# A decode step on one core: VectorE's program as a loop, and one weight load in two parts

## The chip, the core and the metric

The kernel runs on one core of a Trainium2 chip. TensorE (PE) multiplies, VectorE (DVE), ScalarE (ACT) and GpSimd (POOL) work on the operands, and SyncE (SP) issues nearly all DMAs. 16 DMA engines carry the data. The metric is the device time of one execution in microseconds: the median of the kernel before is 292.82 us over three runs (292.77 to 292.93).

## The reference

One decode step of a transformer block for two sequences with one token each, D = 640. x is normalised and multiplied by w_q into 32 heads of 192. Each head attends to the last 2048 of 8192 cached positions, the result goes through w_o, and a feed-forward block with a tanh GELU follows; both blocks add to the residual. Everything is bf16.

```python
W = min(4096, max(256, Sk // 4))                      # 2048
q = (layernorm(x) @ wq).reshape(B, 1, 32, 192).transpose(0, 2, 1, 3)
k, v = k_cache[:, :, Sk - W:, :], v_cache[:, :, Sk - W:, :]
p = softmax(einsum("bhqd,bhkd->bhqk", q, k) * 192 ** -0.5)
h = x + einsum("bhqk,bhkd->bhqd", p, v).transpose(0, 2, 1, 3).reshape(B, 1, 6144) @ wo
n = layernorm(h)
out = h + (gelu(n @ w_gate) * (n @ w_up)) @ w_down
```

Nearly all of the 122 MB that it reads are keys and values (2 x 32 heads x 2048 x 192 x 2 bytes, twice), w_q and w_o. Each byte is used once.

## The kernel before

**Groups.** The 64 pairs of a sequence and a head are worked through in 16 groups of four (g = 0 to 15). A group's keys are one load of 3 MB, its values another, both into a ring of six slots in SBUF. For a group PE transposes the keys in six batches into PSUM (`transposes`, L546), and VectorE (four batches, L573) and ScalarE (two, L569) copy them to `ktr`. Then come the scores (L616) into the PSUM bank `sps`, VectorE's masking and row maximum (L628), its product with a selection (L632), PE's product that spreads the maximum (L635), VectorE's negated maximum `nm` (L637), ScalarE's exponential (L639), PE's turn of the exponentials into columns (L646), VectorE's masked copy of them to `ering` (L653) and PE's product with the values (`pv`, L658). After four groups, a pass J, the sums are divided and multiplied by that pass's quarter of w_o (`z_rows`, `o_rows`, `o_columns`, `oproj`). The products of passes 0 and 1 go to `hrow`: the first by a copy (L723), the second by an addition (L725).

**The tail.** After group 15, `oproj(3)` gives the residual h, PE and VectorE normalise it, and the feed-forward block follows: w_gate (L832, L834), the GELU on VectorE (L835 to L845), w_up in two loads of four and one row blocks (`WUC`, L846), the product `uT` (L850), and w_down in four loads (`WDC`, L851 to L862). VectorE copies the result to `yrow` (L863) and SP writes it out.

**Loads and their order.** `load` puts a load in a queue and `pump` (L336) issues from the head of the queue as soon as the ring slots that it overwrites have been used (`done`). All loads of the ring go through SP in one fixed order: k0, w_q, k1, v0, k2, v1, and so on, w_o's quarters in between, then w_gate, w_up, w_down. The first block of w_gate and x go through ScalarE's queue.

**Order and waits.** `_Prog` records each operation with what it reads and writes, and `resolve` (L129) works out the semaphore waits. PE's program between the first scores and the last group is a loop of four trips, one for a pass (`emit_loop`, L188), in which a wait's value is a constant plus a stride times the trip; parts that do not occur in every pass stand under a condition ("oc", "op", "d0" to "d2"). VectorE has two semaphores (`cls` 0 and 1), so that these strides are constant. The programs of VectorE, ScalarE, GpSimd and SP are written out without a loop. Three calls of `addr_align` (L876, L878, L881) put the next instruction of GpSimd's, VectorE's and ScalarE's program at a chosen place in a block of 128 instructions: place 0, 120 and 0.

The lines that set this:

```python
WUC = ((0, 4), (4, 5))
P.resolve({("dve", 0): 4 * 8, ("dve", 1): 8, ("act", 0): 4 * 3, ("pool", 0): 4})
nc.vector.addr_align(128, 120, 2)
P.emit("dve", nc.vector, sems)
```

Of the kernel before, what the change touches and what calls it, by code (L numbers as in the profile page):

```python
# [6 lines left out]
F32 = mybir.dt.float32  # L7
# [7 lines left out]
NC5 = D // 128  # L15
# [4 lines left out]
F = 1536  # L20
# [3 lines left out]
SCALE = DH ** -0.5  # L24
GELU_2C = 2.0 * 0.7978845608028654


# [23 lines left out]
class _Prog:  # L51
# [3 lines left out]
    def __init__(self):  # L55
        self.ops = []
        self.per = {}
        self.count = {}
        self.w = {}
        self.r = {}  # L60
        self.x = {}
        self.dma_count = {}
        self.seg = self.trip = None
        self.seg_n = 0

    def loop_seg(self, seg=None, trip=None):
        self.seg, self.trip, self.seg_n = seg, trip, 0

    def op(self, eng, fn, R=(), W=(), X=(), dma=None, cls=0):
        o = _Op(eng, cls, fn)  # L70
        deps = []

        def add(y, same_ok):
            if y is None or y is o:
                return
            if y.dma_sem is None and y.eng == eng and dma is None and same_ok:
                return
            deps.append(y)

        for t in R:  # L80
            add(self.w.get(t), eng == "pe")
        for t in W:
            add(self.w.get(t), eng == "pe")
            for y in self.r.get(t, ()):
                add(y, True)
        for t in X:
            for e, y in self.x.get(t, {}).items():
                if e != eng:
                    add(y, True)
        for t in R:  # L90
            self.r.setdefault(t, []).append(o)
        for t in W:
            self.w[t] = o
            self.r[t] = []
        for t in X:
            self.x.setdefault(t, {})[eng] = o
        if dma is not None:
            o.dma_sem = dma
            self.dma_count[dma] = self.dma_count.get(dma, 0) + 16
            o.dma_val = self.dma_count[dma]  # L100
        o.deps = deps
        k = (eng, cls)
        self.count[k] = self.count.get(k, 0) + 1
        o.idx = self.count[k]
        if eng == "pe" and self.seg is not None:
            o.seg, o.slot, o.trip = self.seg, (self.seg, self.seg_n), self.trip
            self.seg_n += 1
        self.per.setdefault(eng, []).append(o)
        self.ops.append(o)
        return o  # L110

    def resolve(self, strides):
# [25 lines left out]
        body = {}  # L138
# [13 lines left out]
        for e, l in self.per.items():  # L152
            n = {}
            for o in l:
                if o.dma_sem is None:
                    n[o.cls] = n.get(o.cls, 0) + (1 if o.need_inc else 0)
                    o.inc_val = n[o.cls]
        self.body = []
        made, at = {}, {}
# [4 lines left out]
        for slot, l in body.items():  # L164
            waits = []
            for key, by in need.get(slot, {}).items():
                S = 16 if key[0] == "d" else strides[key]
                a = max((y.dma_val if y.dma_sem is not None else y.inc_val) - S * t for t, y in by.items())
                for o in l:
                    v = a + S * o.trip  # L170
                    assert 0 < v <= at[slot, o.trip].get(key, 0), (slot, key, o.trip, v, at[slot, o.trip].get(key))
                waits.append((key, a, S))
            self.body.append((l[0].seg, l[0].slot[1], l[0], waits))

# [12 lines left out]

    def emit_loop(self, eng, sems, trips, order):  # L188
        l = self.per["pe"]
        inside = [k for k, o in enumerate(l) if o.slot is not None]  # L190
        self.emit("pe", eng, sems, l[:inside[0]])
        bodies = {}
        for seg, n, o, waits in self.body:
            bodies.setdefault(seg, []).append((n, o, waits))
        with eng.Fori(0, trips) as i:
            def put(items):
                for item in items:
                    if isinstance(item, tuple):
# [7 lines left out]
                        continue  # L206
                    for n, o, waits in sorted(bodies.pop(item), key=lambda q: q[0]):
                        self.emit_one(o, eng, sems, [(key, S * i + a if S else a) for key, a, S in waits])
            put(order)
        assert not bodies, list(bodies)  # L210
        self.emit("pe", eng, sems, l[inside[-1] + 1:])


GRAN = 256
SLOT = 24576
RING = 6 * SLOT
TPG = 64
WDC = ((0, 6), (6, 9), (9, 11), (11, 12))
WUC = ((0, 4), (4, 5))
# [8 lines left out]
def bass_sequential_preLN__sliding_block_cached__geglu_ffn__decode_kernel(  # L228
# [12 lines left out]
    with ExitStack() as ctx:  # L241
# [56 lines left out]
        mrhs = sb("mrhs", [128, 16], BF16)  # L298
        sm = sb("sm", [128, 512], F32)
        nm = sb("nm", [128, 1], F32)  # L300
        zr = sb("zr", [128, 4], F32)
# [30 lines left out]

        def load(key, off, nbytes, src, shape, sem):
            queue.append((key, off, nbytes, src, shape, sem))

        def pump():  # L336
            while queue:
                key, off, nbytes, src, shape, sem = queue[0]
                old = [q for q in live if q[1] < off + nbytes and off < q[1] + q[2]]
                if any(q[0] not in used for q in old):  # L340
                    return
                for q in old:
                    live.remove(q)
                queue.pop(0)
                live.append((key, off, nbytes))
                v = shape(ring[:, off // 2:(off + nbytes) // 2])
                toks = [("ring", x) for x in range(off // GRAN, (off + nbytes + GRAN - 1) // GRAN)]
                where[key] = (v, toks)
                P.op("sp", lambda e, v=v, src=src: e.dma_start(v, src), W=toks + [("sem", sem)], dma=sem)  # L349
# [32 lines left out]
        def load_ffn():  # L382
            load(("wg", 1), K_AT[1], 2 * (NC5 - 1) * F, B_w_gate.rearrange("(p c) f -> p c f", c=NC5)[:, 1:NC5, :],
                 lambda v: v.rearrange("p (c f) -> p c f", f=F), "wg1")
            for i, (c0, c1) in enumerate(WUC):
                load(("wu", i), K_AT[3] + 2 * c0 * F, 2 * (c1 - c0) * F, B_w_up.rearrange("(p c) f -> p c f", c=NC5)[:, c0:c1, :],
                     lambda v: v.rearrange("p (c f) -> p c f", f=F), f"wu{i}")
            wd = B_w_down.rearrange("(q p s) n -> q p s n", p=128, s=6)
# [11 lines left out]

        def pe(fn, R=(), W=(), X=()):
            return P.op("pe", fn, R, W, X)

# [40 lines left out]
        dve(lambda e: e.memset(xnT[:, :, :].rearrange("p a b -> p (a b)").bitcast(I32), 0), W=["xnT"])  # L444
        dve(lambda e: e.memset(lsx[:, :, :], 0.0), W=["lsx"])
        dve(lambda e: e.memset(sps[:, :], 0.0), X=["s"])
        dve(lambda e: e.memset(m1[:, :], 0.0), X=["m1"])
# [128 lines left out]
        def q_rows():  # L576
# [10 lines left out]

            pe(fn, R=["xnT"] + wtoks, X=[("t", 0)])
            done("wq")
# [5 lines left out]
        def q_stationary():  # L595
# [8 lines left out]

            pe(fn, R=["qrow", "selq"], X=["o"])
            dve(lambda e: e.tensor_copy(qs[:, :], ops_[:, 0:384]), W=["qs"], X=["o"])  # L606
# [9 lines left out]
        def scores(g):  # L616
# [9 lines left out]
            if g + 4 < NG:  # L626
                q_masked(g + 4)
            dve(lambda e: e.tensor_tensor_reduce(  # L628
                out=sm[:, :].rearrange("p (u x) -> p u x", u=4), in0=sps[:, :].rearrange("p (u x) -> p u x", u=4),
# [4 lines left out]
        def softmax(g):  # L634
# [4 lines left out]
            act(lambda e: e.activation(out=eexp[:, :], in_=sm[:, :], func=ACT.Exp, bias=nm[:, 0:1], scale=1.0,  # L639
                                       accum_out=zr[:, g % 4:g % 4 + 1]), R=["nm", "sm"],  # L640
                W=["eexp", ("zr", g % 4)])
# [61 lines left out]
        def oproj(J):  # L703
            for i, (k0, k1) in enumerate(wo_parts(J)):
# [16 lines left out]
                done(("wo", J, i))  # L721
            if J == 0:
                dve(lambda e: e.tensor_copy(hrow[0:98, :], m1[0:98, 192:512]), W=["hrow"], X=["m1"])  # L723
            if J == 1:
                dve(tt(hrow[0:98, :], m1[0:98, 192:512], hrow[0:98, :], ALU.add), R=["hrow"], W=["hrow"], X=["m1"])  # L725
# [141 lines left out]

        P.resolve({("dve", 0): 4 * 8, ("dve", 1): 8, ("act", 0): 4 * 3, ("pool", 0): 4})
        sems = {}
        for e, c in (("pe", 0), ("act", 0), ("dve", 0), ("dve", 1), ("pool", 0)):  # L870
            sems[e, c] = ctx.enter_context(nc.semaphore(f"s_{e}{c}"))
        for d in P.dma_count:
            sems["d", d] = ctx.enter_context(nc.semaphore(f"s_{d}"))
        P.emit("sp", nc.sync, sems)
        nc.sync.wait_ge(sems["d", "dout"], 16)
        nc.gpsimd.addr_align(128, 0, 2)  # L876
        P.emit("pool", nc.gpsimd, sems)
        nc.vector.addr_align(128, 120, 2)  # L878
        P.emit("dve", nc.vector, sems)
        P.emit("act", nc.scalar, sems, P.per["act"][:2])  # L880
        nc.scalar.addr_align(128, 0, 2)  # L881
        P.emit("act", nc.scalar, sems, P.per["act"][2:])
        P.emit_loop(nc.tensor, sems, 4, ["a0", (0, None, ["oc"]), "a1", (0, 3, ["op"]), "a2", "b0", "b1", "b2", "c0", "c1", "c2",
                                         (None, 3, ["d0", "d1", "d2"])])

# [27 lines left out]
```

## Time and profile before

| | |
|---|---|
| median of three runs | 292.82 us |
| the profiled execution | 292.81 us |
| its span, first to last instruction | 291.5 us |
| DMA in the span | 122.45 MB, 420 GB/s |
| PE, VectorE, ScalarE, GpSimd busy | 68%, 42%, 26%, 9% |
| mean granted TensorE clock | 0.872 |

The profile is one execution. Busy shares are of the span. The two lines of digits for DMA and GB/s cut the span into 40 equal slices; a DMA digit is the mean busy share of the 16 DMA engines in tenths. Queue q1 is SP's, q10 ScalarE's; "instruction" marks packets that carry program code. The trace also holds each DMA packet by itself, with its queue, size, start and duration, though not the engine that carried it.

### The profile page before, as it was taken

Reading aid. Unit: us, or ns where it says so; the run is one execution under the profiler, and the core shown is the slowest. Engines: PE = TensorE matmul, PEld = TensorE weight load, DVE = VectorE, ACT = ScalarE, POOL = GpSimd, SP = SyncE. Lnnn points to the kernel's source line nnn. Section 1 sums busy time; section 2 is a strip of 40 time slices with the busy share of each in tenths; the row PEclk is TensorE's granted clock in tenths of the full one; section 3 lists DMA queues with packets and bytes.
Section 4 is the critical chain, followed back from the end, with each engine's and each line's share of the span. In section 5 each row is a group of like instructions: output and inputs, shape, how many; then the busy total and the mean of one; then the engine's idle time right before and its main releaser. Section 6 shows DMA issues by size and latency. Waiting matters only on the chain.

```text
span 291.5 us, 4909 instructions
## 1 busy us (share of the span) xinstructions
PE 198.8 (68%) x2141; PEld 147.6 (51%) x2141; DVE 123.1 (42%) x215; ACT 76.9 (26%) x72; POOL 25.4 (9%) x84
## 2 busy tenths in 40 slices
PE   0560858887677377849577478868478778496684
PEld 0450427566375274728374475645465746473341
DVE  5250025455416345535356243635247445253331
ACT  1050013343323122513222123523142334151001
POOL 7820064000000000000000000000000000000000
PEclk9997578999959989997989679999689899788857
DMA  8999999999999999999999999999999999999994
GB/s 311 449 422 428 434 428 432 427 431 428 427 420 442 428 432 432 428 432 432 432 419 444 432 426 432 432 428 432 432 428 432 432 432 428 432 425 414 422 417 172
DMA packets 6507, 122.45 MB, mean 420 GB/s; under 512 B 734, under 2 KB 864, under 8 KB 1504
## 3 DMA queue, kind: packets, MB, share of 16 engines
q1 hardware_dynamic: 6348, 121.90, 97.7%
q10 hardware_dynamic: 148, 0.40, 0.5%
q8 instruction: 7, 0.11, 0.2%
q14 instruction: 4, 0.03, 0.0%
HBM read 122.29 MB, written 0.00 MB: 420 GB/s over the span
## 4 chain that ended last, share of the span: by engine, by line
DMA 63%; PE 24%; DVE 9%; SPq 1%; ACT 1%; issue 1%; POOL 0%; DVEq 0%
DMA ring<-in_A_k_cache_dram 44%; PE tpp L559 16%; DMA ring<-in_A_wq_dram 10%; DMA ring<-in_B_w_down_dram 9%; DVE ktr L573 7%; PE tpp L583 2%; PE sps L620 2%; PE ops L664 2%; SPq L349 1%; DVE ering L414 1%; DVE sm L628 1%; ACT ktr L569 1%; PE m L715 1%; PE m L697 1%; DVE mrhs L410 0%
## 5 line engine op out<-in xcount | busy, mean ns | idle before, releaser
L559 PE MATMUL tpp<-identf,ring 128*128 128x128 f32 x768 | 116.5, 314 | 40.2 <-DMA ring<-in_A_k_cache_dram 26.7
L559 PEld LDWEIGHTS tpp<-identf,ring 128*128 128x128 f32 x768 | 102.9, 163 | 48.6 <-DMA ring<-in_A_k_cache_dram 27.5
L573 DVE COPY ktr<-tpp 128x2048 bf16<-128x2048 bf16 x64 | 78.3, 1224 | 92.5 <-PE tpp L559 92.3
L569 ACT ACTIVATE ktr<-tpp 128x2048 bf16<-128x2048 bf16 x32 | 60.1, 1877 | 95.8 <-PE tpp L559 95.8
L639 ACT ACTIVATE eexp<-sm,nm 128x512 bf16<-128x512 f32 x16 | 11.5, 722 | 72.0 <-DVE nm L637 72.0
L620 PE MATMUL sps<-ktr,rq 128*16 128x512 bf16 x384 | 25.7, 401 | 1.1 <-POOL rq L414 1.1
L664 PE MATMUL ops<-ring,ering 128*32 128x384 bf16 x512 | 25.0, 340 | 0.0
L628 DVE CUSTOM_DVE_ANT_1 sm<-sps,mska 128x512 f32<-128x512 f32 x16 | 11.1, 691 | 27.0 <-PE sps L620 27.0
L414 POOL TENSOR_TENSOR rq<-qs,mask 128x96 bf16<-128x96 bf16 x16 | 5.6, 356 | 175.7 <-PE sps L620 153.6
L664 PEld LDWEIGHTS ops<-ring,ering 128*32 128x32 bf16 x512 | 12.7, 99 | 8.5 <-issue 2.0
L620 PEld LDWEIGHTS sps<-ktr,rq 128*16 128x16 bf16 x384 | 8.8, 89 | 14.3 <-issue 5.4
L635 PEld LDWEIGHTS m<-mrhs,pm 128*128 128x128 bf16 x16 | 1.5, 96 | 23.0 <-DVE mrhs L410 23.0
L635 PE MATMUL m<-mrhs,pm 128*128 128x16 bf16 x16 | 2.9, 184 | 14.9 <-DVE mrhs L410 14.9
L583 PE MATMUL tpp<-ring,xnT 128*32 128x384 bf16 x80 | 6.2, 502 | 9.1 <-DMA ring<-in_A_wq_dram 9.1
L583 PEld LDWEIGHTS tpp<-ring,xnT 128*32 128x32 bf16 x80 | 3.4, 144 | 11.8 <-issue 9.4
L414 DVE TENSOR_TENSOR ering<-m,mask 128x256 bf16<-128x256 f32 x16 | 6.6, 414 | 1.3 <-PE m L648 1.3
L606 DVE CAST qs<-ops 128x384 bf16<-128x384 f32 x1 | 0.6, 556 | 15.6 <-PE ops L601 15.6
L697 PE MATMUL m<-selb,orow 128*128 128x2 bf16 x48 | 3.5, 199 | 5.3 <-DVE ering L414 4.6
L697 PEld LDWEIGHTS m<-selb,orow 128*128 128x128 bf16 x48 | 3.1, 161 | 6.0 <-DVE ering L414 5.0
L648 PE MATMUL m<-sel,eexp 128*128 128x64 bf16 x64 | 4.6, 196 | 1.2 <-ACT eexp L639 1.2
L414 DVE TENSOR_TENSOR orow<-m,wm 128x1536 bf16<-128x1536 f32 x3 | 5.3, 1750 | 0.0
L648 PEld LDWEIGHTS m<-sel,eexp 128*128 128x128 bf16 x64 | 4.3, 102 | 1.6 <-DVE nm L637 1.3
(126 smaller groups left out, 89.1 us busy)
## 6 DMA issues: line engine op xcount, KB each, us to landing
ring<-in_A_k_cache_dram SPq DMA_DIRECT2D x16, 3072.0 KB, 29.4
ring<-in_A_v_cache_dram SPq DMA_DIRECT2D x16, 3072.0 KB, 25.1
ring<-in_A_wq_dram SPq DMA_DIRECT2D x1, 7680.0 KB, 28.7
ring<-in_A_wo_dram SPq DMA_DIRECT2D x4, 1920.0 KB, 21.5
ring<-in_B_w_gate_dram SPq DMA_DIRECT2D x1, 1536.0 KB, 31.2
ring<-in_B_w_up_dram SPq DMA_DIRECT2D x1, 1536.0 KB, 21.9
ring<-in_B_w_down_dram SPq DMA_DIRECT2D x1, 960.0 KB, 24.3
ring<-in_B_w_down_dram SPq DMA_DIRECT2D x1, 480.0 KB, 25.0
```

Of the source, the lines that this page charges most:

```text
L414: return lambda e: e.tensor_tensor(out=out, in0=a, in1=b, op=op)
L559: ins = e.transpose(tpp[bi][:, 512 * j + 128 * u:512 * j + 128 * (u + 1)], kv[:, off:off + 128], identf[:, :])
L569: act(lambda e, dst=dst, bv=bv: e.activation(out=dst, in_=bv, func=ACT.Copy), W=[("kt", half, k)], X=both)
L573: dve(lambda e, dst=dst, bv=bv: e.tensor_copy(dst, bv.rearrange("p (a x) -> p a x", a=2)), W=[("kt", half, k)], X=both, cls=0)
L583: ins = e.matmul(tps[0][32 * r:32 * (r + 1), 0:384], lhsT=xnT[:, c, 32 * J:32 * (J + 1)], rhs=wq[:, c, 1536 * J + 384 * r:1536 * J + 384 * ...
L620: ins = e.matmul(sps[32 * ch:32 * ch + 16, :], lhsT=rq[:, g % 4, k, :], rhs=ktr[:, k // 2, 1024 * ch + k % 2:1024 * (ch + 1):2], start=(k ...
L628: dve(lambda e: e.tensor_tensor_reduce(out=sm[:, :].rearrange("p (u x) -> p u x", u=4), in0=sps[:, :].rearrange("p (u x) -> p u x", u=4), ...
L635: pe(lambda e: e.matmul(m2[:, 256:272], lhsT=pm[:, :], rhs=mrhs[:, :], start=True, stop=True), R=["pm", "mrhs"], X=["m2"])
L639: act(lambda e: e.activation(out=eexp[:, :], in_=sm[:, :], func=ACT.Exp, bias=nm[:, 0:1], scale=1.0, accum_out=zr[:, g % 4:g % 4 + 1]), R= ...
L648: ins = e.matmul(o, lhsT=eexp[:, 128 * u:128 * (u + 1)], rhs=sel64[:, :], start=True, stop=True)
L664: ins = e.matmul(ops_[32 * r:32 * (r + 1), 0:384], lhsT=ering[:, g % 4, t, :], rhs=vv[:, 384 * t:384 * (t + 1)], start=(g % 4 == 0 and t < 4),
L697: ins = e.matmul(m2[:, 2 * kk:2 * kk + 2], lhsT=orow[:, :, kk:DH:12], rhs=selb[:, :], start=True, stop=True)
```

## The change

VectorE's program gets a loop of four trips like PE's, and the three `addr_align` calls leave. For the loop each of VectorE's operations must be the same in every trip. So the first addition to `hrow` is an addition too, on a `hrow` that GpSimd sets to zero at the start. A small memset (`gate`) ahead of L628 takes the wait for the scores, and the exponential waits for `gate` as well. PE's operations that do not occur in every trip get a semaphore of their own (`cls` 1).

The second load of w_up (one row block of 128 partitions, 384 KB) becomes two loads, first partitions 100 to 127, then 0 to 99, each with its own semaphore. PE's four products with it wait for both.

```diff
+LOOPED = ("pe", "dve")
+RARE = ("oc", "op")
...
     def op(self, eng, fn, R=(), W=(), X=(), dma=None, cls=0):
+        if eng == "pe" and self.seg in RARE:
+            cls = 1
...
-        if eng == "pe" and self.seg is not None:
-            o.seg, o.slot, o.trip = self.seg, (self.seg, self.seg_n), self.trip
-            self.seg_n += 1
+        if eng in LOOPED and self.seg is not None:
+            n = self.seg_n.get(eng, 0)
+            o.seg, o.slot, o.trip = self.seg, (eng, self.seg, n), self.trip
+            self.seg_n[eng] = n + 1
...
+        for l in body.values():
+            for o in l:
+                if o.eng == "pe" and o.need_inc and o.trip > l[0].trip:
+                    n = (o.inc_val - l[0].inc_val) // (o.trip - l[0].trip)
+                    assert strides.setdefault(o.key(), n) == n, (o.key(), n)
...
+WUP = 100
...
+        gate = sb("gate", [128, 1], F32)
...
+        def part_toks(off, nbytes, part):
+            return [("ring", x, part) for x in range(off // GRAN, (off + nbytes + GRAN - 1) // GRAN)]
...
+                if part is not None:
+                    P.op("sp", lambda e, v=v, src=src: e.dma_start(v, src), W=part_toks(off, nbytes, part) + [("sem", sem)], X=toks, dma=sem)
+                    continue
...
-                load(("wu", i), K_AT[3] + 2 * c0 * F, 2 * (c1 - c0) * F, B_w_up.rearrange("(p c) f -> p c f", c=NC5)[:, c0:c1, :],
-                     lambda v: v.rearrange("p (c f) -> p c f", f=F), f"wu{i}")
+                off, nb = K_AT[3] + 2 * c0 * F, 2 * (c1 - c0) * F
+                src = B_w_up.rearrange("(p c) f -> p c f", c=NC5)[:, c0:c1, :]
+                if i == 0:
+                    load(("wu", i), off, nb, src, lambda v: v.rearrange("p (c f) -> p c f", f=F), f"wu{i}")
+                    continue
+                for p0, p1 in ((WUP, 128), (0, WUP)):
+                    load(("wu", i), off, nb, src[p0:p1], lambda v, p0=p0, p1=p1: v[p0:p1, :].rearrange("p (c f) -> p c f", f=F),
+                         f"wu{i}{p0}", p0)
...
+        pool(lambda e: e.memset(hrow[:, :], 0.0), W=["hrow"])
...
+            dve(lambda e: e.memset(gate[:, :], 0.0), W=["gate"], X=["s"], cls=0)
...
-                                       accum_out=zr[:, g % 4:g % 4 + 1]), R=["nm", "sm"],
+                                       accum_out=zr[:, g % 4:g % 4 + 1]), R=["nm", "sm", "gate"],
...
-            if J == 0:
-                dve(lambda e: e.tensor_copy(hrow[0:98, :], m1[0:98, 192:512]), W=["hrow"], X=["m1"])
-            if J == 1:
+            if J < 2:
                 dve(tt(hrow[0:98, :], m1[0:98, 192:512], hrow[0:98, :], ALU.add), R=["hrow"], W=["hrow"], X=["m1"])
...
-        P.resolve({("dve", 0): 4 * 8, ("dve", 1): 8, ("act", 0): 4 * 3, ("pool", 0): 4})
+        P.resolve({("dve", 0): 4 * 9, ("dve", 1): 8, ("act", 0): 4 * 3, ("pool", 0): 4})
...
-        nc.gpsimd.addr_align(128, 0, 2)
         P.emit("pool", nc.gpsimd, sems)
-        nc.vector.addr_align(128, 120, 2)
-        P.emit("dve", nc.vector, sems)
-        P.emit("act", nc.scalar, sems, P.per["act"][:2])
-        nc.scalar.addr_align(128, 0, 2)
-        P.emit("act", nc.scalar, sems, P.per["act"][2:])
...
+        P.emit("act", nc.scalar, sems)
+        order = ["a0", (0, None, ["oc"]), "a1", (0, 3, ["op"]), "a2", "b0", "b1", "b2", "c0", "c1", "c2", (None, 3, ["d0", "d1", "d2"])]
+        P.emit_loop("dve", nc.vector, sems, 4, order)
+        P.emit_loop("pe", nc.tensor, sems, 4, order)
```

More of the change, by code (lines that the diff above doesn't have):

```diff
@@ L63, in __init__ @@
         self.seg = self.trip = None
-        self.seg_n = 0
+        self.seg_n = {}
     def loop_seg(self, seg=None, trip=None):
-        self.seg, self.trip, self.seg_n = seg, trip, 0
+        self.seg, self.trip, self.seg_n = seg, trip, {}
     def op(self, eng, fn, R=(), W=(), X=(), dma=None, cls=0):
+        if eng == "pe" and self.seg in RARE:
+            cls = 1
         o = _Op(eng, cls, fn)
@@ L172, in resolve @@
                 waits.append((key, a, S))
-            self.body.append((l[0].seg, l[0].slot[1], l[0], waits))
+            self.body.append((l[0].seg, l[0].slot[2], l[0], waits))
     def emit_one(self, o, eng, sems, waits):
@@ L186, in emit, with emit_loop @@
             self.emit_one(o, eng, sems, [(y.key(), y.dma_val if y.dma_sem is not None else y.inc_val) for y in o.waits])
-    def emit_loop(self, eng, sems, trips, order):
-        l = self.per["pe"]
+    def emit_loop(self, name, eng, sems, trips, order):
+        l = self.per[name]
         inside = [k for k, o in enumerate(l) if o.slot is not None]
-        self.emit("pe", eng, sems, l[:inside[0]])
+        self.emit(name, eng, sems, l[:inside[0]])
         bodies = {}
         for seg, n, o, waits in self.body:
-            bodies.setdefault(seg, []).append((n, o, waits))
+            if o.eng == name:
+                bodies.setdefault(seg, []).append((n, o, waits))
         with eng.Fori(0, trips) as i:
@@ L206, in put @@
                         continue
-                    for n, o, waits in sorted(bodies.pop(item), key=lambda q: q[0]):
+                    for n, o, waits in sorted(bodies.pop(item, ()), key=lambda q: q[0]):
                         self.emit_one(o, eng, sems, [(key, S * i + a if S else a) for key, a, S in waits])
@@ L210, in emit_loop @@
         assert not bodies, list(bodies)
-        self.emit("pe", eng, sems, l[inside[-1] + 1:])
+        self.emit(name, eng, sems, l[inside[-1] + 1:])
 GRAN = 256
@@ L331, in bass_sequential_preLN__sliding_block_cached__geglu_ffn__decode_kernel, with load @@
         where, live, queue, used = {}, [], [], set()
-        def load(key, off, nbytes, src, shape, sem):
-            queue.append((key, off, nbytes, src, shape, sem))
+        def load(key, off, nbytes, src, shape, sem, part=None):
+            queue.append((key, off, nbytes, src, shape, sem, part))
+        def part_toks(off, nbytes, part):
+            return [("ring", x, part) for x in range(off // GRAN, (off + nbytes + GRAN - 1) // GRAN)]
         def pump():
             while queue:
-                key, off, nbytes, src, shape, sem = queue[0]
+                key, off, nbytes, src, shape, sem, part = queue[0]
                 old = [q for q in live if q[1] < off + nbytes and off < q[1] + q[2]]
-                if any(q[0] not in used for q in old):
+                if any(q[0] not in used and q[0] != key for q in old):
                     return
@@ L385, in load_ffn @@
             for i, (c0, c1) in enumerate(WUC):
-                load(("wu", i), K_AT[3] + 2 * c0 * F, 2 * (c1 - c0) * F, B_w_up.rearrange("(p c) f -> p c f", c=NC5)[:, c0:c1, :],
-                     lambda v: v.rearrange("p (c f) -> p c f", f=F), f"wu{i}")
+                off, nb = K_AT[3] + 2 * c0 * F, 2 * (c1 - c0) * F
[6 more added lines that the diff above has]
+                         f"wu{i}{p0}", p0)
+                where["wu", i] = (ring[:, off // 2:(off + nb) // 2].rearrange("p (c f) -> p c f", f=F), part_toks(off, nb, WUP) + part_toks(off, nb, 0))
             wd = B_w_down.rearrange("(q p s) n -> q p s n", p=128, s=6)
@@ L399, in act, with pe @@
             return P.op("act", fn, R, W, X)
-        def pe(fn, R=(), W=(), X=()):
-            return P.op("pe", fn, R, W, X)
+        def pe(fn, R=(), W=(), X=(), cls=0):
+            return P.op("pe", fn, R, W, X, cls=cls)
         def pool(fn, R=(), W=(), X=()):
@@ L586, in fn @@
                 return ins
-            pe(fn, R=["xnT"] + wtoks, X=[("t", 0)])
+            pe(fn, R=["xnT"] + wtoks, X=[("t", 0)], cls=1)
             done("wq")
@@ L603, in fn @@
                 return ins
-            pe(fn, R=["qrow", "selq"], X=["o"])
+            pe(fn, R=["qrow", "selq"], X=["o"], cls=1)
             dve(lambda e: e.tensor_copy(qs[:, :], ops_[:, 0:384]), W=["qs"], X=["o"])
@@ L865, in bass_sequential_preLN__sliding_block_cached__geglu_ffn__decode_kernel @@
              dma="dout")
-        P.resolve({("dve", 0): 4 * 8, ("dve", 1): 8, ("act", 0): 4 * 3, ("pool", 0): 4})
+        P.resolve({("dve", 0): 4 * 9, ("dve", 1): 8, ("act", 0): 4 * 3, ("pool", 0): 4})
         sems = {}
-        for e, c in (("pe", 0), ("act", 0), ("dve", 0), ("dve", 1), ("pool", 0)):
+        for e, c in (("pe", 0), ("pe", 1), ("act", 0), ("dve", 0), ("dve", 1), ("pool", 0)):
             sems[e, c] = ctx.enter_context(nc.semaphore(f"s_{e}{c}"))
@@ L875, in bass_sequential_preLN__sliding_block_cached__geglu_ffn__decode_kernel @@
         nc.sync.wait_ge(sems["d", "dout"], 16)
-        nc.gpsimd.addr_align(128, 0, 2)
         P.emit("pool", nc.gpsimd, sems)
-        nc.vector.addr_align(128, 120, 2)
-        P.emit("dve", nc.vector, sems)
-        P.emit("act", nc.scalar, sems, P.per["act"][:2])
-        nc.scalar.addr_align(128, 0, 2)
-        P.emit("act", nc.scalar, sems, P.per["act"][2:])
-        P.emit_loop(nc.tensor, sems, 4, ["a0", (0, None, ["oc"]), "a1", (0, 3, ["op"]), "a2", "b0", "b1", "b2", "c0", "c1", "c2",
-                                         (None, 3, ["d0", "d1", "d2"])])
+        P.emit("act", nc.scalar, sems)
+        order = ["a0", (0, None, ["oc"]), "a1", (0, 3, ["op"]), "a2", "b0", "b1", "b2", "c0", "c1", "c2", (None, 3, ["d0", "d1", "d2"])]
+        P.emit_loop("dve", nc.vector, sems, 4, order)
+        P.emit_loop("pe", nc.tensor, sems, 4, order)
 _INS = ['A_x', 'A_k_cache', 'A_v_cache', 'A_wq', 'A_wo', 'B_x', 'B_w_gate', 'B_w_up', 'B_w_down']
```

## The prediction

> **What bounds the kernel now.** I read the page's DMA parts first, then the chain, then the end of the run in stretches, then the trace's packet records.
>
> ```profile
> span 291.5 us, 4909 instructions
> ...
> DMA  8999999999999999999999999999999999999994
> ...
> q1 hardware_dynamic: 6348, 121.90, 97.7%
> q10 hardware_dynamic: 148, 0.40, 0.5%
> q8 instruction: 7, 0.11, 0.2%
> q14 instruction: 4, 0.03, 0.0%
> ```
>
> The reader is to see that the 16 DMA engines are full from the second slice to the last, and that eleven packets of the span carry program code: seven of 16 KB on q8, four of 8 KB on q14.
>
> The chain of waits, in order of time, ends so:
>
> ```profile
> 263.24 25.34 DMA ring<-in_B_w_down_dram
> 288.57 0.04 issue
> 288.62 0.74 PE m L857 x12
> 289.38 0.33 DVE yrow L863
> ```
>
> SP issued w_down 25 us before it landed. The packet records give that lead for each load: the shortest between issue and first packet is 6.4 us (k11, issued at 177.32, first packet at 183.71). The queue is never empty, so a slower VectorE costs nothing inside the loop until a group is more than 6 us late. What counts is when the last engine is done, and the stretches at the end show that the 16 do not finish together (columns: stretch, length, the engines' busy time, clock, DMA share, GB/s):
>
> ```profile
> 284.00:286.00 2.00, 1.31 (x18) 0.38 (x10) 0.84 (x4) 0.80 (x2) 0.00 (x0) 0.72 1.00 406
> 286.00:286.50 0.50, 0.38 (x3) 0.22 (x2) 0.08 (x1) 0.00 (x0) 0.00 (x0) 1.00 0.96 369
> 286.50:287.00 0.50, 0.25 (x16) 0.28 (x20) 0.14 (x1) 0.00 (x0) 0.00 (x0) 1.00 0.61 236
> 287.00:287.50 0.50, 0.34 (x20) 0.14 (x8) 0.00 (x0) 0.00 (x0) 0.00 (x0) 1.00 0.49 195
> 287.50:288.00 0.50, 0.19 (x12) 0.18 (x12) 0.00 (x0) 0.00 (x0) 0.00 (x0) 1.00 0.42 159
> 288.00:288.60 0.60, 0.20 (x12) 0.00 (x0) 0.00 (x0) 0.00 (x0) 0.00 (x0) 0.95 0.25 85
> ```
>
> The share falls from 1.00 to 0.25 over 2.5 us: ten engines at work after 286.5, four after 288. The work after 286.0, spread evenly, would end at 286.0 + (0.48 + 0.31 + 0.25 + 0.21 + 0.15) = 287.40. So 288.53 - 287.40 = 1.1 us is the most that any balancing of engines can give.
>
> I followed the packets engine by engine (a packet starts where one of the last size ended). Over 286.30 us the engines finish at:
>
> ```
> code packet of 16 KB passed (35.2, 55.5, 65.1, 76.2, 93.6, 275.1 us): 1.58 1.77 1.82 1.90 1.90 2.16
> code packets of 8 KB passed: 2.23 (5.2 and 170.3 us), 1.11 (1.8 and 6.2 us)
> the other eight: 0.06 0.10 0.12 0.19 0.23 0.29 0.51 0.78
> ```
>
> The 16 KB packet at 35.2 put its engine back by 1.48 us (0.19 to 1.67 behind the first), the 8 KB packet at 170.3 by 0.98 (1.22 to 2.20). VectorE had then started 121 of its 221 instructions, ScalarE 42 of 73 and GpSimd 81 of 84, so I take that code for VectorE's.
>
> **The change, part by part.**
>
> *VectorE's loop.* It folds 3 of 4 trips away, so VectorE's program gets shorter. If the 170.3 packet goes, its engine ends at 2.23 - 0.98 = 1.25 and the last one is 2.16: 0.07 us gained. If code is fetched at another time instead, 0. If each trip fetches, see rival 2.
>
> New on VectorE are about one register operation a wait, one memset a group, branches. PE's records show 0.032 us for a register operation and 0.21 to 0.35 for the loop's branch; a VectorE memset of one column took 0.06 (eps_t). Over a trip that is at most 50 x 0.032 + 4 x 0.06 + some 1 us of branches = 3 us, beside the 6.4 us lead. It can show only in the last trip. There nine VectorE steps lie between k15's landing at 252.1 and the end: 0.06 + 9 x 0.032 + 0.35 = 0.7 us if nothing is hidden, 0 if the sequencer runs ahead of the queue. The cover is at the tail. uT ends at 286.64, and PE's 48 w_down matmuls take 0.63 + 0.39 + about 0.35 us without waits, so compute alone would be done at 288.0 where PE ends at 289.36: 1.36 us. I take 0.1 of it as used; without that cover the 0.7 would show in full.
>
> *Alignments.* Three leave, with a branch each (VectorE's at 0.75, 0.05 us). They lie beside the wait for w_q until 30.1. Where code is cut into packets moves with them: the early 8 KB packets (0.5 to 0.6 us each) may stay or go, on engines that are not last.
>
> *GpSimd's memset of hrow,* 320 columns: between 0.19 (108 columns) and 1.81 us (2048); I take 0.3. GpSimd's q_masked waits 22 us for qs later on; that hides it. The added ops for hrow in trip 0 are 0.480 for 0.478 us. SP issues one load more, 0.43 us by the neighbouring rows, at 262, with w_down queued behind it for 19 us: nothing. The second semaphore of PE and the assertion cost no time on an engine.
>
> *The split.* The 384 KB load has 128 rows of 3072 bytes, eight for each engine, 0.119 us a row. The trace shows one load of fewer rows, x with two: its semaphore got 14 at once at 1.98 and then one step for each of two engines (5.66, 6.49). So such loads run on fewer engines, in whole rows. Equal shares of 100 rows need at most ten engines, of 28 at most fourteen. Then ten engines carry 10 + 2 rows for 8 (+0.47 us), four carry 2 (-0.71), two none (-0.95). That six engines shed rows, and six passed PE's code, is what decides me. [...] Shed by the six: 2.16 - 0.71 = 1.45 at most. Laden: 0.78 + 0.47 = 1.25 of the eight, 1.11 + 0.47 = 1.58, and the 170.3 engine 1.25 + 0.47 = 1.72, or about 1.2 if its early packet is gone too. The new last lies between 1.25 and 1.72; I take 1.56, near the laden engine that needs fewest assumptions: -0.67 us. The bounds: the even spread above gives -1.1; the laden engine of 2.23 with its fetch left in place gives +0.47.
>
> [...]
>
> *Sum.* -0.67 at the last landing; landing to end (288.97 to 291.49) is untouched. Against the profiled execution's 292.81 (span 291.5, 1.3 around it; the median is 292.82): 292.14, say **292.15**.
>
> **The rivals.**
>
> *1. The rows moved wait where they land.* The moved rows still go to the same partitions, while the late engines write theirs at 27 GB/s (24576 bytes in 0.909 us). If partitions take no more than that, the late engines get nothing back (last 2.16) and the laden ten run their ten rows at down to half pace: 1.11 + 0.47 + 10 x 0.119 = 2.77, or 1.72 + 1.19 = 2.91. Change -0.07 to +0.68, and +1 where waits chain: 292.7 to 293.8, middle 293.3. For it: in the trace every engine keeps the same pace in each 128-row load, and no load shows several engines going to few partitions, so nothing says that they can. Against: nothing says that they cannot.
> [...]
>
> *2. The loop fetches its code in every trip* (the other side). If VectorE's body crosses the edge of an 8 KB packet and falls out, each fetch costs its engine 0.98. One more than hoped already gives 1.25 + 0.98 + 0.47 = 2.70, slower than 2.23; four give 5.6: +0.5 to +3.4, 293.3 to 296.2. It decides from the first fetch. Against: PE's loop fetched in its first trip (55.5 to 93.6) and then not until 275.1.
> [...]
>
> *3. The wrong engines shed.* If the engine of 275.1 is among the ten: 1.58 + 0.47 = 2.05, -0.18: 292.6. If the late six are laden: 2.16 + 0.47, +0.40: 293.2.
>
> *4. Compute takes over*, with more than 0.7 us of loop cost in the last trip: 292.4 to 292.9.
>
> **How the numbers follow.** About 0.2% (0.59 us) is what a measurement of this kernel can tell from no change. Forecast: 0.52, its own range 291.8 to 292.4, of which 0.05 falls within 0.2%. Rival 1: 0.22 (0.15 slower, 0.07 same). Rival 2: 0.12, slower. Rival 3: 0.12 (0.08 same, 0.04 slower). Rival 4: 0.02, same. Faster 0.47, same 0.22, slower 0.31. The range 291.8 to 293.6 leaves out most of rival 2 and the top of rival 1.
>
> **What would show it.** The loop: no code packet near 170, none more than one trip's worth; if VectorE's code comes four times, rival 2. The split: w_up's two parts counted on 14 and 10 engines; DMA share above 0.8 until 287.5, then a steep fall, last landing near 288.3. Rows of 3072 bytes at 0.119 us; at 0.15 or more, rival 1. L857's last wait still on w_down; if PE waits for uT instead, rival 4. What would make it wrong: a laden engine that is already late, or moved rows that are slower than the rows they replace.

## The result and the profile after

The changed kernel takes 295.17 us (median of six runs, 294.79 to 295.34) against 292.81 us for the kernel before (six runs, 292.75 to 292.93). The ratio is 1.0076, with a 95% interval of 1.0066 to 1.0086: slower by 0.8%. The forecast was 292.15, a gain. The profiled execution took 294.83 us with a span of 293.4.

These are lines of the page of the changed kernel that answer to those shown of before: the span, the 40 slices of DMA share and of GB/s, and the queues.

```profile
span 293.4 us, 5095 instructions
...
DMA  8997999999999999999999999999999999999994
GB/s 322 429 520 338 428 429 429 431 442 436 431 408 449 429 429 429 432 429 429 429 425 433 429 429 427 429 429 432 429 429 432 436 432 432 436 432 410 429 303 163
...
q1 hardware_dynamic: 6356, 121.90, 97.8%
q10 hardware_dynamic: 148, 0.40, 0.4%
q8 instruction: 7, 0.11, 0.2%
q14 instruction: 3, 0.02, 0.0%
```

The share of busy time at the end is the same digits as before. The GB/s are not: the last slice but one (278.7 to 286.1) moved 303 where its neighbours moved 410 to 430. The same slice of the kernel before:

```profile
GB/s 311 449 422 428 434 428 432 427 431 428 427 420 442 428 432 432 428 432 432 432 419 444 432 426 432 432 428 432 432 428 432 432 432 428 432 425 414 422 417 172
```

There it is 417 (276.9 to 284.2). So the DMA engines were occupied and moved a quarter less. The stretches show where (columns: stretch, length, busy time of PE, PEld, DVE, ACT, POOL, granted clock, DMA share, GB/s; a packet counts whole in the stretch in which it starts, so a share can pass 1.00 and the rate of a short stretch is rough). First the two stretches of before that the prediction did not show, then those of after:

```profile
280.00:282.00 2.00, 2.00 (x30) 0.90 (x22) 0.14 (x2) 0.46 (x2) 0.00 (x0) 0.50 0.99 409
282.00:284.00 2.00, 1.79 (x23) 0.71 (x19) 1.06 (x4) 0.00 (x0) 0.00 (x0) 0.50 0.99 404
```

```profile
280.00:282.00 2.00, 2.00 (x26) 0.89 (x22) 0.36 (x1) 0.46 (x2) 0.00 (x0) 0.50 1.09 322
282.00:284.00 2.00, 0.88 (x7) 0.46 (x3) 0.98 (x5) 0.03 (x1) 0.00 (x0) 0.50 1.01 236
284.00:286.00 2.00, 1.45 (x16) 0.32 (x16) 0.66 (x3) 0.20 (x1) 0.00 (x0) 0.50 0.95 290
...
288.00:288.60 0.60, 0.40 (x3) 0.10 (x1) 0.16 (x1) 0.00 (x0) 0.00 (x0) 0.50 0.92 361
288.60:289.50 0.90, 0.79 (x24) 0.65 (x24) 0.06 (x1) 0.00 (x0) 0.00 (x0) 0.50 0.57 213
289.50:290.50 1.00, 0.78 (x20) 0.25 (x12) 0.00 (x0) 0.00 (x0) 0.00 (x0) 0.50 0.14 47
```

From 280.6, when the first row of the split load starts, to 286 the share stays near 1.0 while the rate falls to 236 GB/s; after 286.5 it is back. The fall at the end is no steeper than before. From the last stretch above 0.9 to the last packet it took 2.0 us before (286.5 to 288.53) and takes 1.8 now (288.6 to 290.40). The idle time of an engine in those tails, one minus the share times the length, sums to 1.14 us before (from 286.0, to 288.53) and 1.20 now (from 288.0, the last stretch counted to 290.4). So nothing was evened out.

The packet records name the slow rows. Each load has its own row size:

```
row size, load                            before: median, max ns    after: median, max ns    extra time, us (after - before)
12288  w_gate and w_up's first load       462   1007                464   1007                  7.9
 3072  w_up's second load (the split)     121    133                214    308                 10.4
 7680  w_down's first load                295    308                374    646                 13.3
 3840, 2560, 1280  the other w_down       149, 102, 55 (medians)    149, 102, 55 (medians)      0.1
landing: w_up's first load                283.30                    284.34
         w_up's second load               284.26                    284.84 (100 to 127), 286.42 (0 to 99)
         w_down, four loads               286.61 287.77 288.57 288.97   288.54 289.71 290.49 290.88
last packet ends                          288.53                    290.40
```

The extra time of a row is its duration less the usual one. Over all rows after 264 us it comes to 2.14 us per engine (the sum divided by 16) after and 0.16 before: 1.98 more, and the last packet ends 1.87 later. The slow rows are of the size of the whole loss. Two thirds of the extra time fell on rows that the change did not touch: w_up's first load, which is queued ahead of the split one and yet lands 1.04 us later, and w_down's first, behind it.

What follows the landing is as it was. The chain of after ends so:

```profile
263.00 27.49 DMA ring<-in_B_w_down_dram
290.53 0.74 PE m L885 x11
```

And the timeline of after (start, length, engine, line, operation, in brackets the idle time before it and what ended it) shows PE waiting for each part:

```profile
284.38 1.45 PE L836 MATMUL ops<-ring,hnT 128*2 128x384 bf16 x16 [1.31 <-DMA ring<-in_B_w_up_dram]
286.46 0.49 PE L836 MATMUL ops<-ring,hnT 128*2 128x384 bf16 x4 [0.62 <-DMA ring<-in_B_w_up_dram]
288.44 0.22 DVE L442 TENSOR_TENSOR uT<-tpp,ga 128x24 bf16<-128x24 f32 x1 [3.47 <-PE tpp L845]
290.53 0.70 PE L885 MATMUL m<-ring,uT 128*17 128x160 bf16 x12 [0.20 <-DMA ring<-in_B_w_down_dram]
```

w_up's products wait for the two parts, but the last wait is on w_down, which came late by itself. From its landing to the end of the span it was 2.5 us before (288.97 to 291.5) and is 2.5 now (290.88 to 293.4).

### The profile page after: what moved, and what is told of

It reads as the page before. It is cut to its first block, busy times and chain, and to the rows that moved or that the text cites. A ratio compares the mean times of both kernels' runs of the same rounds, so it can differ in the third digit from the quotient of the medians.

```text
span 293.4 us, 5095 instructions
## 1 busy us (share of the span) xinstructions
PE 197.6 (67%) x2141; PEld 145.3 (50%) x2141; DVE 122.8 (42%) x231; ACT 76.9 (26%) x72; POOL 25.7 (9%) x85
## 4 chain that ended last, share of the span: by engine, by line
DMA 73%; PE 19%; DVE 3%; issue 2%; SPq 2%; ACT 1%; DVEq 0%
DMA ring<-in_A_k_cache_dram 54%; PE tpp L588 14%; DMA ring<-in_A_wq_dram 10%; DMA ring<-in_B_w_down_dram 9%; DVE ktr L602 2%; PE tpp L612 2%; SPq L370 2%; PE ops L694 1%; DVE ering L442 1%; PE m L745 1%; ACT ktr L598 1%; PE m L727 1%; SPq L367 0%; PE m L885 0%; PE m L708 0%
## 5 line engine op out<-in xcount | busy, mean ns | idle before, releaser
L588 PE MATMUL tpp<-identf,ring 128*128 128x128 f32 x768 | 113.8, 310 | 42.1 <-DMA ring<-in_A_k_cache_dram 27.8
L588 PEld LDWEIGHTS tpp<-identf,ring 128*128 128x128 f32 x768 | 100.2, 160 | 50.4 <-DMA ring<-in_A_k_cache_dram 29.0
L708 PE MATMUL m<-zr,zsel 128*128 128x4 f32 x8 | 1.7, 289 | 5.1 <-DVE ering L442 5.1
```

The lines of the kernel that those rows point to most:

```text
L588: ins = e.transpose(tpp[bi][:, 512 * j + 128 * u:512 * j + 128 * (u + 1)], kv[:, off:off + 128], identf[:, :])
```

## The experiments

The theories. **P**: several engines write into the same few partitions and wait for each other there (the prediction's first rival). **L**: VectorE's loop, with its code packets. **S**: the unequal shares, ten engines with too much. **N**: more loads, more and smaller rows. The answer to one question, where rows may go without a wait, changed on the way: P began as "partitions close together", which the strides of six and of eight contradict, and what sets the cuts that cost apart from those that don't was not shown.

This table has what each kernel gave. Each ratio is against runs of the kernel before made beside it (medians 292.81 to 293.02). "Extra" is the extra row time after 264 us per engine, as above; "last packet" is against 288.53 of before (for the kernels that have the loop, 288.52 of the loop alone).

```
kernel                                 time (runs)   ratio to before [95%]      extra   last packet
changed kernel                         295.17 (6)    1.0076 [1.0066, 1.0086]    2.14    +1.88
split alone                            295.78 (4)    1.0102 [1.0086, 1.0117]    2.46    +2.69
loop alone                             292.78 (11)   0.9995 [0.9986, 1.0004]    0.17    -0.01
w_up's second load cut at 64           295.19 (4)    1.0074 [1.0057, 1.0091]    2.50    +2.65
w_up's second load in column halves    293.00 (10)   1.0003 [0.9993, 1.0012]    0.17    +0.08
w_o's last load cut at 64              300.05 (2)    1.0244 [1.0206, 1.0282]    7.19    +8.52
  in 32:96, 0:32, 96:128               297.97 (2)    1.0173 [1.0130, 1.0215]    5.78    +5.98
  in column halves                     292.96 (8)    1.0002 [0.9992, 1.0013]    0.18    +0.08
  every fourth partition               292.89 (9)    1.0002 [0.9992, 1.0012]    0.16    -0.01
  even and odd partitions              292.98 (11)   1.0002 [0.9993, 1.0011]    0.17    +0.07
  every eighth partition               299.01 (5)    1.0210 [1.0196, 1.0224]    6.02    +5.81
loop, strides that empty six engines   294.57 (5)    1.0052 [1.0039, 1.0066]    1.74    +1.56
loop, strides that halve six engines   293.63 (11)   1.0022 [1.0013, 1.0031]    1.04    +0.62
```

### The two halves of the change

The split alone: the kernel before with

```diff
+WUP = 100
...
+                for p0, p1 in ((WUP, 128), (0, WUP)):
+                    load(("wu", i), off, nb, src[p0:p1], lambda v, p0=p0, p1=p1: v[p0:p1, :].rearrange("p (c f) -> p c f", f=F),
+                         f"wu{i}{p0}", p0)
```

> The kernel before with w_up's second load in two parts, and nothing else. Theory P (the parts' writes queue where they land: several engines at the same few partitions): the whole loss is here, 2.0 to 2.6 us over the kernel before, 294.8 to 295.4; DMA busy but at some 290 GB/s around 285 us, rows of 7680 bytes that take over 0.4 us where 0.29 is normal. Theory L (VectorE's loop and its code packets cost the time): no loss beyond the 0.47 us of the laden engines, 292.8 to 293.3. Theory S (only the unequal shares of rows count, each row at its usual 0.119 us): 292.3 to 293.3.

The loop alone: the changed kernel with w_up's second load in one piece,

```diff
-                for p0, p1 in ((WUP, 128), (0, WUP)):
-                    load(("wu", i), off, nb, src[p0:p1], lambda v, p0=p0, p1=p1: v[p0:p1, :].rearrange("p (c f) -> p c f", f=F),
-                         f"wu{i}{p0}", p0)
+                load(("wu", i), off, nb, src, lambda v: v.rearrange("p (c f) -> p c f", f=F), f"wu{i}")
```

> The changed kernel with w_up's second load as one load again: VectorE's loop, no alignments. P: no loss; in the trace of the changed kernel the last engine ended w_o's last load at 275.04 us, in the kernel before at 275.45, so 0.4 us are gained: 292.4 (292.3 to 292.8). L: 294.5 to 295.2. S: as P.

The split alone is slower by 1.0%, the loop alone can't be told from before. The stretches of the split alone, then of the loop alone:

```profile
280.00:282.00 2.00, 1.73 (x20) 0.80 (x22) 0.64 (x4) 0.18 (x1) 0.00 (x0) 0.50 1.04 330
282.00:284.00 2.00, 1.80 (x23) 0.81 (x15) 0.62 (x1) 0.28 (x2) 0.00 (x0) 0.50 1.00 220
284.00:286.00 2.00, 1.30 (x19) 0.36 (x17) 1.21 (x6) 0.22 (x1) 0.00 (x0) 0.50 0.98 250
```

```profile
280.00:282.00 2.00, 2.00 (x26) 0.89 (x22) 0.19 (x1) 0.47 (x2) 0.00 (x0) 0.50 0.97 404
282.00:284.00 2.00, 1.80 (x23) 0.68 (x15) 0.98 (x3) 0.00 (x0) 0.00 (x0) 0.50 1.02 415
```

220 GB/s at a share of 1.00 against 415: the sag belongs to the split. L falls. Two expectations were missed by a little: the split alone came out above P's 295.4, and the 0.4 us that the loop alone was to gain did not show (292.78). Why the split costs somewhat more without the loop (2.9 against 2.4 us) was not settled.

### Is it the shares, or where the rows go?

Here w_o's last load (128 rows of 15360 bytes, 1.9 MB) is cut instead, in the kernel before: its rows are five times as long, so a wait shows better, and in the first two 16 engines can share the rows evenly. `load` gets a list of cuts, and `pump` issues one DMA for each:

```diff
+WO3 = (lambda t: t[0:64], lambda t: t[64:128])
...
+                if more:
+                    extra = [("part", sem, m) for m in range(1, len(more))]
+                    for m, cut in enumerate(more):
+                        P.op("sp", lambda e, v=cut(v), src=cut(src): e.dma_start(v, src),
+                             W=(toks if m == 0 else [extra[m - 1]]) + [("sem", sem, m)], dma=sem + "abc"[m])
+                    where[key] = (v, toks + extra)
+                    continue
...
+                     more=WO3 if J == 3 else ())
```

> The kernel before with w_o's last load (128 rows of 15360 bytes, 4.6 us) in two parts, partitions 0 to 63 and 64 to 127. Each engine still carries 8 rows in all. [...] S and L: 292.8 to 293.0, since shares are equal and the program is the same.

The second kernel has the same with

```diff
+WO3 = (lambda t: t[32:96], lambda t: t[0:32], lambda t: t[96:128])
```

> As w64, in three parts: partitions 32 to 95, 0 to 31, 96 to 127. Again 8 rows for each engine. [...] If smaller parts alone were slow (fewer rows, more counts), more than w64. S and L: 292.8 to 293.0.

The cut at 64 cost 7.1 us in the median of its two runs (298.85 and 301.26), where S and L expected 292.8 to 293.0. The stretches of the slower one, which was profiled:

```profile
270.00:272.00 2.00, 0.93 (x8) 0.62 (x4) 1.18 (x3) 0.00 (x0) 0.00 (x0) 0.95 0.86 169
272.00:274.00 2.00, 0.00 (x0) 0.00 (x0) 1.20 (x1) 0.00 (x0) 0.00 (x0) 0.90 1.06 207
274.00:276.00 2.00, 0.00 (x0) 0.00 (x0) 0.00 (x0) 0.00 (x0) 0.00 (x0) 0.50 1.09 230
276.00:278.00 2.00, 1.94 (x26) 0.73 (x26) 0.00 (x0) 0.00 (x0) 0.00 (x0) 0.50 0.88 189
```

Half the rate, at shares of 0.86 to 1.09, in all stretches from 270 to 282: 169 to 230 GB/s, where the kernel before moved 395 to 436. The parts 32:96, 0:32, 96:128 cost 5.1 us (296.62 and 299.32), not more than the cut at 64, as it would be if smaller parts alone were slow. The stretches of the slower run:

```profile
270.00:272.00 2.00, 1.01 (x14) 0.54 (x16) 1.35 (x1) 0.00 (x0) 0.00 (x0) 1.00 1.41 361
272.00:274.00 2.00, 1.60 (x36) 1.12 (x28) 0.59 (x2) 0.00 (x0) 0.00 (x0) 1.00 0.83 131
274.00:276.00 2.00, 0.00 (x0) 0.00 (x0) 0.00 (x0) 0.00 (x0) 0.00 (x0) 0.97 0.93 161
```

These three belong together, since slow rows that start before 272 still run behind it: 218 GB/s in the mean. The part that spans the middle half was not slow by itself. The packet records have the fifty rows of 15360 bytes that start from 269.0 to 270.85, all but eight at most from that part, at 0.57 to 0.59 us, the pace of a whole load (0.578 in the kernel before). The rows that start from 270.9 on are slow, up to 1.85 us. That is when the first engine is done with the middle half (271.52 by the semaphore) and goes on to partitions 0 to 31, while the last one is done with it only at 277.59. Engines stand 2.4 us apart at the start (269.18 to 271.55), so that parts run side by side. Parts that 16 engines can share evenly plainly are not free for that.

### Is it the number of loads and rows?

The same load in column halves (256 rows of 7680 bytes), and in four parts of every fourth partition (the same rows as whole, 32 in a part):

```diff
+WO3 = (lambda t: t[:, 0:6], lambda t: t[:, 6:12])
```

> The kernel before with w_o's last load in two parts by columns: each part has all 128 partitions, rows of 7680 bytes. P (writes queue where several engines go to the same few partitions): every engine writes the partitions that it always writes, nothing to queue for: 292.8 to 293.1. Theory N (it is the number of DMAs or of rows in each that costs): a good part of w64's 7 us.

```diff
+WO3 = (lambda t: t[0:128:4], lambda t: t[1:128:4], lambda t: t[2:128:4], lambda t: t[3:128:4])
```

> The kernel before with w_o's last load in four parts, each of every fourth partition (0, 4, ... 124, then 1, 5, ... and so on): two rows an engine in each part, and each part spread over the whole of the partitions. P: far less than w64 (+7.1) and w32 (+5.1), between 0 and 2.5 us, 292.8 to 295.3, since no part crowds one region; what is left depends on which engine takes which row. N (more and smaller DMAs): more than w64, over 299.9.

Both cost nothing (1.0002 each). The stretch of the four parts beside that of the cut at 64 above:

```profile
270.00:272.00 2.00, 1.54 (x12) 0.94 (x4) 0.62 (x2) 0.00 (x0) 0.00 (x0) 0.60 1.01 430
272.00:274.00 2.00, 1.30 (x27) 0.55 (x26) 1.76 (x1) 0.00 (x0) 0.00 (x0) 1.00 1.00 424
```

Four loads run at 424 GB/s where two ran at 207. N falls.

The two kernels on w_up's second load itself, cut in equal halves of partitions, and in column halves (rows of 1536 bytes):

```diff
-WUP = 100
+WUP = 64
```

> As the kernel with the split alone, cut at partition 64 instead of 100: two parts of 64 rows, which 16 engines can share evenly, so that no engine gets more than its 8 rows. P: the parts still crowd, 128 rows at about twice 0.119 us, 8 x 0.119 = 1 us or somewhat more: 293.7 to 295. S (it was the unequal shares, 12, 2 and 0 rows): 292.8 to 293.1.

```diff
+WU1 = (lambda t: t[:, :, 0:768], lambda t: t[:, :, 768:1536])
```

> The kernel before with w_up's second load in two parts by columns, all 128 partitions in each, rows of 1536 bytes. P: 292.8 to 293.1 (128 more packet starts over 16 engines). N: 294 or more.

Equal halves lose 2.2 us (1.0074), as much as the changed kernel: its rows of 3072 bytes take 208 ns in the median, 376 at most. S is not needed. Column halves cost nothing (1.0003).

### Can the shares be moved without the crowding?

If rows only wait where partitions lie close together, strides should give what the change was to give. So w_up's second load was cut again in the loop kernel, with parts of 20 rows, taken to run on ten engines as the changed kernel's 100 did, so that six engines get no rows, or half:

```diff
+WU1 = (slice(0, 115, 6), slice(1, 116, 6), slice(2, 117, 6), slice(3, 118, 6), slice(4, 119, 6), slice(5, 120, 6), slice(120, 128))
```

> The changed kernel with its loop and without alignments, but w_up's second load cut another way: six loads of every sixth partition (20 rows each, so ten engines with two rows each) and one of partitions 120 to 127. Ten engines then carry about 12 rows and six carry none, as the change wanted, and neighbouring partitions are not crowded. In the kernel with the loop alone the six late engines end 1.57 to 2.22 us behind the first, the other ten at most 1.39. Theory 'engines' (the balance works where the place is not crowded): rows of 3072 bytes keep 0.12 us, the six gain 0.95 (0.62 to 1.27), the ten lose about 0.47 (at most 1.86), so the last engine ends some 0.35 earlier: 292.4 to 292.6. Theory 'places' (the partitions take no more than their one engine's pace, whoever brings the rows): rows at 0.15 or more, last landing no earlier: 292.8 to 293.5. If crowding comes back in full: 294 or more, with 0.2 us a row.

```diff
+WU1 = (slice(0, 128, 2), slice(1, 116, 6), slice(3, 118, 6), slice(5, 120, 6), slice(121, 128, 2))
```

> The same with only half of the rows moved: one load of the 64 even partitions (16 engines, four rows each), three of every sixth partition (20 rows each, ten engines) and one of the last four odd partitions. Ten engines carry about ten rows for eight, six carry four. Theory 'engines': the six late ones gain 0.47 (last 1.75 instead of 2.22), the ten lose 0.24 (at most 1.63): last engine some 0.47 earlier, 292.3 to 292.5, a little ahead of the load with all rows moved. Theory 'places': 292.8 to 293.5 with rows at 0.15 or more.

Neither gained. The first cost 1.6 us (1.0052), with 200 ns a row, the second 0.6 (1.0022), with 154. The stretch of each:

```profile
282.00:284.00 2.00, 1.80 (x23) 0.73 (x11) 0.62 (x1) 0.14 (x1) 0.00 (x0) 0.50 1.00 245
```

```profile
282.00:284.00 2.00, 1.81 (x23) 0.79 (x15) 0.62 (x1) 0.22 (x2) 0.00 (x0) 0.50 0.99 283
```

Twenty partitions spread over 115 are not crowded, and still the rate sagged to 245. "Close together" is therefore not the condition. Theory "engines" fell. "Places" named the direction but not the size: the first kernel came out as "crowding in full" had it (294 or more, 0.2 us a row), the second just above the 293.5 of "places".

### Is it the spread?

What the free cuts have in common can't be read from the trace, which doesn't say which engine carried a packet. Two more cuts of w_o's last load, which by "close together" should both cost nothing:

```diff
+WO3 = (lambda t: t[0:128:2], lambda t: t[1:128:2])
```

> The kernel before, with w_o's last load (128 rows of 15360 bytes) as two loads, the even partitions and the odd ones. Same rows, same number of loads and 64 rows each, as in the cut at partition 64 that cost 7.1 us. [...] Theory 'crowding' (a part is slow where its partitions lie close together): 0.

```diff
+WO3 = tuple(lambda t, r=r: t[r:128:8] for r in range(8))
```

> The same load in eight parts of every eighth partition (16 rows each, one row for each engine). [...] Theory 'crowding': rows at 0.58 us, 292.9 to 293.1, as for four parts of every fourth partition. If the number of loads costs by itself, a gap between parts and rows at 0.58.

Even and odd partitions, then every eighth partition:

```profile
270.00:272.00 2.00, 1.53 (x16) 0.76 (x8) 0.62 (x2) 0.00 (x0) 0.00 (x0) 0.70 1.03 438
272.00:274.00 2.00, 1.36 (x28) 0.56 (x26) 1.75 (x1) 0.00 (x0) 0.00 (x0) 1.00 0.98 416
```

```profile
270.00:272.00 2.00, 1.53 (x12) 1.14 (x4) 0.62 (x2) 0.00 (x0) 0.00 (x0) 0.50 1.03 215
272.00:274.00 2.00, 1.43 (x16) 0.45 (x18) 1.50 (x1) 0.00 (x0) 0.00 (x0) 0.50 1.01 230
```

Two parts of 64 rows by stride run at 416 to 438 GB/s, where two parts of 64 rows cut at 64 ran at 207. Eight parts, each spread as widely as can be, run at 215 and 230 and cost 6.1 us. Nor does their number explain it: the extra row time is 6.02 us per engine, the last packet 5.81 later, so the loss is in slow rows, not in gaps between the loads. Neither closeness nor spread decides.

What does stays open. A stride of two or four cost nothing (1.0002 each), one of eight 2.1%, and in w_up's load the strides of six 0.5% and 0.2%; no run shows why. And each cut also changes which rows of the source are read together; no kernel here tells the reading side from the writing side.

No kernel here was faster than the kernel before by more than the noise: the lowest ratio is 0.9995 [0.9986, 1.0004].

## Why the prediction was wrong

**The term that failed** is the price of the rows in the split: "Then ten engines carry 10 + 2 rows for 8 (+0.47 us), four carry 2 (-0.71), two none (-0.95)", at 0.119 us a row. That took a row's time as a property of its engine. Measured, the split's rows took 205 ns in the mean and up to 308, and the rows that met them were slowed as well. In place of -0.67 came +1.91 at the last landing (288.97 to 290.88), +1.87 at the last packet, and +2.02 in the profiled execution (294.83 for 292.81); the medians differ by 2.36, since the profiled execution is the second quickest of the six.

**The first rival showed its mark, and was priced too low.** The mark, rows at 0.15 us or more, was passed. Its price, -0.07 to +0.68, "and +1 where waits chain", took only the ten moved rows of a laden engine at half pace. The table of rows shows what it left out: of 31.6 us of extra time (7.9 + 10.4 + 13.3) the split's own rows hold 10.4, a third. The other two thirds lie on the loads before and behind it. Why those were slowed with them was not shown.

**The shares came out as worked.** w_up's parts were counted on 14 and 10 engines: the semaphore of partitions 100 to 127 jumped at once (261.87) and then took 14 steps, that of 0 to 99 (262.25) ten. Which engines these were no run shows: that the ten are among the fourteen, and that the late ones shed rows, were terms of the -0.67 without a measurement.

**No balance followed.** DMA share above 0.8 held longer than forecast, until 288.6, but then fell over 1.8 us, not steeply; six engines that shed rows did not get ahead by it.

**VectorE's loop: -0.07 was forecast,** by way of the code packet at 170.3 leaving. The loop alone gave -0.01 at the last packet and a ratio of 0.9995 [0.9986, 1.0004], which allows both -0.07 and nothing. A late packet stayed: with the loop q14 still has one at 178 (178.33 in the changed kernel, 178.66 in the loop alone), and one at 61.5 where the early ones had been at 1.8 to 6.2. Which engine's code these carry is not shown. Three packets in the span in place of four, and none that returns with the trips, so the second rival did not happen.

**What hid the rest held.** SP's added issue took 0.47 us (0.43 expected) with 27 us between w_down's issue and its landing; compute was not the last wait, so the fourth rival is out. The third, the wrong engines shed, can't be told: with rows that wait the question has no effect that shows.

**The alternative was there to be weighed higher.** The prediction wrote that no load of the trace has several engines going to few partitions. An operation that the trace never shows was given the usual row's price for the forecast, and 0.22 for anything else. In the kernel before, 128 rows of 3072 bytes took 0.121 us each in the median and 0.133 at most; that says nothing of a load of fewer partitions.

## What to carry to other kernels

Loads over all partitions ran at 395 to 453 GB/s here (the kernel before, stretches from 264 to 286). To cut such a load for an earlier start, cut columns, or take every second or fourth partition: these cost nothing here (1.0002 or 1.0003), and every cut into ranges of partitions that was tried did (1.0074 to 1.0244). Look at GB/s beside the DMA share: an engine with a slow row counts as busy, and a stretch at 1.0 share and half the rate is the mark of it (1.06 at 207 GB/s in the cut at 64). Cuts meant to move rows from late engines to early ones helped in none of the four kernels that tried it (1.0022 to 1.0102), and in the changed kernel the load queued ahead landed 1.04 us later too.

## What was not expected of the hardware

- w_o's last load cut at partition 64, into two parts of 64 rows, halved the rate: 207 GB/s where the four parts of every fourth partition ran at 424, and 7.1 us more on a load that takes 4.6 us by itself (128 rows of 0.578 us on 16 engines).
- A wide spread was as bad: every eighth partition ran at 215 to 230 GB/s, every fourth at 424 to 430.
- A load was slowed by one that was issued after it: w_up's first load landed at 284.34 in place of 283.30, though SP issued it 0.37 us ahead of the split.
- The granted clock was 0.50 in all stretches of the changed kernel from 286.0 on, where the kernel before shows 1.00 from 286.0 to 288.0. As the last wait is on w_down, the end does not show a cost of it.
